# Three expert blocks of a fused attention and mixture-of-experts kernel, rewritten from float32 products into split float32r products

## The chip, the cores and the metric

The kernel runs on one core of one Trainium2 chip. The metric is device time in microseconds of one execution (lower is better). TensorE multiplies and adds into PSUM; ScalarE (ACT in rows), VectorE (DVE) and GpSimd (POOL) do the elementwise work; SyncE (SP) issues most of the transfers. In the rows PE is TensorE's matmuls and PEld its weight loads.

## The reference

Three layers follow each other. The change lies in the second, the top-1 mixture of experts:

```python
# attention: B=2, H=8, S=768, D=64, a query sees the keys of its own cluster -> x: 1536 x 512
logits = x @ w_gate                      # 8 experts
expert_idx = np.argmax(logits, axis=1)
gate_w = softmax(logits)[arange, expert_idx]
for e in range(8):
    mask = expert_idx == e
    h = np.maximum(x[mask] @ w1[e], 0.0) # w1[e]: 512 x 1024
    out[mask] = gate_w[mask, None] * (h @ w2[e])   # w2[e]: 1024 x 512
h = out @ w_in                           # 512 x 2048
g = np.maximum(h, 0) + alpha * np.minimum(h, 0)
return g @ w_out                         # 2048 x 512
```

## The kernel before

The program has three stages: attention, the eight experts, and the dense layer. The tokens of each expert have been gathered into one block. Expert 0 is block 0 (208 rows); the others follow by falling size, with fixed capacities of 306, 216, 200, 192, 176, 168 and 128 rows (`CAPS`). A block is computed transposed: the rows are the columns that a matmul streams, and the weights are what it holds.

The experts run as one loop over steps `g` (`NG` is 64, eight steps `f` to a block). Step g emits `l1(blk, f)`, which makes 128 of the 1024 hidden columns from four products over d, evacuated by a ReLU on ScalarE into `h`; then `l2` of the step two back (`LAG` is 2), which adds that piece of `h` into four PSUM banks; then small side work, at f of 6 the transposes of the next block's rows (`x_transp`), and last the conversions of the dense layer's weights. `l1` has two PSUM banks (`bank(f % 2)`), so step g+2 can't start before the evacuation of step g. At the end of a block `y_evac` copies the four output banks out. The schedule is manual: each engine runs its instructions in the order in which the program emits them.

Operands of the experts are float32; a float32 matmul shows as two records in the trace, each with its own weight load. The dense layer already works with split operands: a value is `hi` (rounded to float32r by a ScalarE copy) plus `lo` (the rest, by a VectorE subtraction), and three float32r products, hi by hi, hi by lo and lo by hi, take the place of one float32 product.

Expert weights arrive as 1 MB chunks, four to a block, in a ring of four slots on SyncE's queue. `wload()` is called when a chunk has been used up and loads the one four places on. The weights of the dense layer arrive as raw 512 KB pieces on the same queue and are converted in steps of one piece (`conv_run`): step k emits the load of piece k, `conv_abs` of piece k-1 (ScalarE, reads the raw piece), `conv_bits` of piece k-2 and `conv_lo` of piece k-4 (VectorE, five instructions), and `conv_hi` of piece k-3 (ScalarE). Two raw buffers exist, so the load of piece k waits for `conv_bits` of piece k-2. The table `PER` says how many conversion steps each block has; the rest (32 pieces, 36 steps) fall one to a step into the start of the dense layer. Their results live in `m2w_t[c]`, pairs of 128x2048 tiles; the first five pairs have memory of their own that is empty until the conversions fill it.

Of the kernel before, what the change touches and what calls it, by code (L numbers as in the profile page):

```python
# [90 lines left out]
def tile_cluster_attention_moe(ctx: ExitStack, tc: tile.TileContext, qk, kk, v, cen, cenr, gate, mw, m2w,  # L91
                               alpha, consts, table, pos, zeros, out):
    nc = tc.nc
# [94 lines left out]
    def conv_run(pool, ks):  # L188

        for k in ks:  # L190
            at = lambda lag: 0 <= k - lag < NCA
# [470 lines left out]
    def at(j, w, f, *a):  # L662
        todo.setdefault((j, w), []).append((f, a))
# [193 lines left out]
    ps = bank(0)[:, 448:448 + E]  # L857
# [169 lines left out]
    def reg(ap, engs, hi):  # L1027
        return nc.values_load(ap, engines=engs, min_val=0, max_val=hi)
# [45 lines left out]


    more = nc.values_load(ovi[0:1, 0, 3:4], min_val=0, max_val=NSEL)
    with tc.For_i(0, more, 1):  # L1077
# [7 lines left out]
        for d in range(4):  # L1085
            ps = bank(2 + d % 2)
# [3 lines left out]
        for f in range(8):  # L1090
# [5 lines left out]
            ps = bank(f % 2)  # L1096
# [169 lines left out]
```

## Time and profile before

| | |
|---|---|
| time, three runs | 716.39, 716.99, 718.03 us (median 716.99) |
| the profiled execution | 717.95 us |
| its span, first to last instruction | 716.2 us |
| TensorE busy (matmul records) | 695.7 us, 97% |
| TensorE weight loads busy | 562.8 us, 79% |
| VectorE busy | 419.0 us, 59% |
| ScalarE busy | 283.5 us, 40% |
| mean granted TensorE clock | 0.989 of full speed |

The profiled execution lies 0.96 us above the median, and 1.75 us of its time are outside the span. A busy share is a mean over three stages with different limits; the expert stage lies between 264 and 446 us of the span, and only it is rewritten. A matmul record's length contains the drain of the array, so what a matmul costs in a stream is the distance between the starts of two records, not the length of one.

### The profile page before, as it was taken

The page shows a single profiled execution, that of the slowest core. Times are in us where ns is not written, and L with a number is a line of the kernel's source. Part 1 is how long each engine was busy: PE and PEld are TensorE (multiplying, and loading weights), DVE is VectorE, ACT ScalarE, POOL GpSimd, SP SyncE. Part 2 cuts the span into 40 slices and gives each one's busy share as a digit, 9 for nine tenths or more (in the row PEclk, how much of TensorE's full clock was granted, in tenths as well). Part 3 has the DMA queues.
Part 4 walks back from the last instruction along what each step waited for, and adds up shares of the span by engine and source line. Part 5 has one row for each costly group of instructions (what it writes and reads, how often), then busy time and mean ns, then how long its engine had stood idle before and what let it go on. Part 6 is the DMA issues. An engine that isn't in the chain of part 4 may idle for free. (4 is left out here: it accounts for less than half of the span.)

```text
span 716.2 us, 10510 instructions
## 1 busy us (share of the span) xinstructions
PE 695.7 (97%) x3966; PEld 562.8 (79%) x3966; DVE 419.0 (59%) x781; ACT 283.5 (40%) x589; POOL 62.4 (9%) x67
## 2 busy tenths in 40 slices
PE   7899999999999999999999998999999999999996
PEld 3676767666667689779999998888888888888885
DVE  7877778788886561686532104799654433543342
ACT  5877877857576412343332213333121111221111
POOL 4220202222220120000000000000002000020002
PEclk8999999999999999999999999899999999999999
DMA  8346667425430027978879775132001000010001
GB/s 268 95 155 190 243 214 243 132 83 135 122 81 1 17 98 224 254 268 273 292 262 260 282 251 121 60 117 89 1 0 60 1 0 1 0 59 1 0 1 59
DMA packets 24763, 89.75 MB, mean 125 GB/s; under 512 B 6818, under 2 KB 8365, under 8 KB 20519
## 3 DMA queue, kind: packets, MB, share of 16 engines
q1 hardware_dynamic: 19515, 72.83, 33.0%
q0 software_dynamic: 3216, 12.60, 5.1%
q10 hardware_dynamic: 1980, 3.63, 1.7%
q8 instruction: 32, 0.52, 0.3%
q14 instruction: 20, 0.16, 0.1%
HBM read 75.06 MB, written 11.35 MB: 121 GB/s over the span
## 5 line engine op out<-in xcount | busy, mean ns | idle before, releaser
L1153 ACT ACTIVATE gh<-gg 128x512 fp32r<-128x512 f32 x48 | 30.4, 632 | 195.7 <-DVE gg L1152 189.5
L401 DVE TENSOR_REDUCE sm<-PS 128x1 f32<-128x768 f32 x96 | 91.9, 957 | 14.9 <-PE PS L395 14.5
L411 ACT ACTIVATE P<-PS,sm 128x768 f32<-128x768 f32 x96 | 86.5, 901 | 32.1 <-DVE sm L401 32.1
L910 PE MATMUL PS<-x,w 128*128 128x208 f32 (+7 forms) x512 | 96.8, 332 | 0.0
L925 PE MATMUL PS<-h,w 128*128 128x208 f32 (+7 forms) x512 | 96.5, 332 | 0.0
L925 PEld LDWEIGHTS PS<-h,w 128*128 128x128 f32 x512 | 83.7, 190 | 4.4
L910 PEld LDWEIGHTS PS<-x,w 128*128 128x128 f32 x512 | 83.7, 190 | 4.2
L425 PEld LDWEIGHTS PS<-cst,P 128*128 128x128 f32 x576 | 63.4, 140 | 29.9 <-ACT P L411 16.8
L425 PE MATMUL PS<-cst,P 128*128 128x128 f32 x576 | 82.6, 278 | 3.3 <-ACT P L411 1.5
L1151 DVE TENSOR_SCALAR gg<-PS,alph 128x512 f32<-128x512 f32 x48 | 36.0, 749 | 80.8 <-PE PS L1143 80.6
L1141 PE MATMUL PS<-x2hi,w2h 128*128 128x512 f32 x192 | 76.0, 396 | 2.7 <-ACT x2hi L1129 2.7
L1142 PE MATMUL PS<-x2lo,w2h 128*128 128x512 f32 x192 | 75.9, 395 | 0.0
L1143 PE MATMUL PS<-x2hi,w2l 128*128 128x512 f32 x192 | 75.7, 394 | 0.0
L428 DVE COPY PT<-PS 128x384 f32<-128x384 f32 x96 | 53.0, 552 | 38.5 <-PE PS L425 38.5
L1170 PE MATMUL PS<-w2h,gh 128*128 128x512 f32 x192 | 74.7, 389 | 0.0
L1171 PE MATMUL PS<-w2l,gh 128*128 128x512 f32 x192 | 74.7, 389 | 0.0
L1172 PE MATMUL PS<-w2h,gl 128*128 128x512 f32 x192 | 74.7, 389 | 0.0
L394 PE MATMUL PS<-KA,QA 128*128 128x512 f32 x192 | 73.8, 384 | 0.0
L434 PE MATMUL PS<-PT,V 128*64 128x384 f32 (+1 forms) x432 | 72.4, 462 | 0.0
L395 PE MATMUL PS<-KB,QB 96*128 96x512 f32 x192 | 61.3, 341 | 0.0
L427 ACT ACTIVATE PT<-PS 128x384 f32<-128x384 f32 x96 | 46.7, 486 | 28.6 <-PE PS L425 27.1
L912 ACT ACTIVATE h<-PS 128x208 f32<-128x208 f32 (+7 forms) x64 | 21.3, 333 | 79.2 <-PE PS L910 79.1
(170 smaller groups left out, 861.9 us busy)
## 6 DMA issues: line engine op xcount, KB each, us to landing
w<-in_mw SPq DMA_DIRECT2D x32, 1024.0 KB, 7.3
raw<-in_m2w SPq DMA_DIRECT2D x32, 512.0 KB, 4.1
R<-in_qk SPq DMA_DIRECT2D x7, 768.0 KB
KA<-in_kk POOLq DMA_DIRECT2D x7, 768.0 KB
Xs<-in_zeros SPq DMA_DIRECT2D x8, 614.4 KB
QA<-QB SPq DMA_DIRECT2D x16, 192.0 KB, 2.6
V<-in_v SPq DMA_DIRECT2D x8, 384.0 KB
KB<-KA SPq DMA_DIRECT2D x7, 384.0 KB, 4.1
```

Source lines behind the costliest of these rows:

```text
L394: nc.tensor.matmul(ps[:, ks], st["QA"][:, hh, q0:q0 + P], st["KA"][:, hh, ks], start=True, stop=False)
L401: nc.vector.tensor_reduce(smt[s], psS[s % 2], AX.X, ALU.max, negate=True)
L411: nc.scalar.activation(Pt, psS[s % 2], AF.Exp, bias=smt.pop(s)[:, 0:1], accum_out=RS[:, tt, h:h + 1])
L425: nc.tensor.transpose(v4[:, kt // 3, kt % 3, :], Pt[:, kt * P:(kt + 1) * P], idf)
L910: nc.tensor.matmul(ps, w[:, d, fs], x[:, d, :], start=d == 0, stop=d == 3)
L925: nc.tensor.matmul(yps[blk][o][:, 0:nb], w[:, f % 4, o * P:(o + 1) * P], h, start=f == 0, stop=f == 7)
L1141: nc.tensor.matmul(ps, whi[:, d, fs], xhi[:, d, :], start=d == 0, stop=False)
L1142: nc.tensor.matmul(ps, whi[:, d, fs], xlo[:, d, :], start=False, stop=False)
L1143: nc.tensor.matmul(ps, wlo[:, d, fs], xhi[:, d, :], start=False, stop=d == 3)
L1170: nc.tensor.matmul(y, gh[:, c], whi[:, f % 4, :], start=f == 0, stop=False)
L1171: nc.tensor.matmul(y, gh[:, c], wlo[:, f % 4, :], start=False, stop=False)
L1172: nc.tensor.matmul(y, gl[:, c], whi[:, f % 4, :], start=False, stop=f == 15)
```

## The change

Block 1 (306 rows) goes from one float32 product to three float32r products. Its four weight chunks are split into hi and lo by `wsplit`, a quarter chunk at a time, into the pairs `m2w_t[1]` to `m2w_t[4]`, at the steps that the table `SPLITS` lists (7 to 13); its rows are split in `x_transp`, its hidden values in `l1s`.

Blocks 2 and 3 (216 and 200 rows) keep the hi and lo halves of their rows side by side, so that one float32r product of hi weights with both halves (432 or 400 columns) and one of lo weights with the hi half (216 or 200 columns) do the work. The two halves of the result are added afterwards, in `l1r` and in `y_evac`. Their weights are split in rolling pieces: `wroll` writes a 128x512 piece of hi and of lo for the next step, into eight pieces that lie in `m2w_t[2][1]` and `m2w_t[3][1]`.

`PER` changes from (3, 8, 4, 3, 2, 1, 0, 2) to (2, 2, 1, 1, 5, 5, 2, 2): 20 conversion steps in the expert stage where there were 23. The weight register of block g+2 is read a block earlier, since chunks are used up sooner. Blocks 0 and 4 to 7 keep their float32 code.

```diff
+        if blk in ROLL:
+            x = xts[blk] = ROLL[blk][0][:, 0:8 * nb].rearrange("p (d s n) -> p d s n", d=4, s=2)
+        elif blk == SPL:
+            xs1[:] = [xtp.tile([P, 4, CMAX], F32R, name=f"x{n}_{blk}", tag="x") for n in ("hi", "lo")]
...
+            if blk in ROLL:
+                xv = x[:, dn * g:dn * (g + 1), :, :]
+                nc.scalar.activation(xv[:, :, 0, :], pv, AF.Copy)
+                nc.vector.tensor_sub(xv[:, :, 1, :], pv, xv.bitcast(F32)[:, :, 0, :])
+            elif blk == SPL:
+                for k in range(dn):
+                    d = dn * g + k
+                    nc.scalar.activation(xs1[0][:, d, 0:nb], pv[:, k], AF.Copy)
+                    nc.vector.tensor_sub(xs1[1][:, d, 0:nb], pv[:, k], xs1[0].bitcast(F32)[:, d, 0:nb])
...
+    def wsplit(k, pieces):
+        hi, lo = m2w_t[1 + k]
+        w = wslots[4 * SPL + k]
+        for i in pieces:
+            c = slice(512 * i, 512 * (i + 1))
+            nc.scalar.activation(hi[:, c], w[:, c], AF.Copy)
+            nc.vector.tensor_sub(lo[:, c], w[:, c], hi.bitcast(F32)[:, c])
+        if pieces[-1] == 3:
+            wload()
+
+    def l1s(f):
...
+        for d in range(4):
+            nc.tensor.matmul(ps, whi[:, d, fs], xhi[:, d, :], start=d == 0, stop=False)
+            nc.tensor.matmul(ps, whi[:, d, fs], xlo[:, d, :], start=False, stop=False)
+            nc.tensor.matmul(ps, wlo[:, d, fs], xhi[:, d, :], start=False, stop=d == 3)
...
+        nc.scalar.activation(hh, ps, AF.Relu)
+        nc.vector.scalar_tensor_tensor(hl, ps, 0.0, hh.bitcast(F32), ALU.max, ALU.subtract)
...
+    ROLL = {2: m2w_t[2], 3: (m2w_t[4][0],)}
+    gran = [m2w_t[2][1][:, 512 * i:512 * (i + 1)] for i in range(4)]
+    gran_lo = [m2w_t[3][1][:, 512 * i:512 * (i + 1)] for i in range(4)]
+    hjoin = m2w_t[3][0]
+
+    def wroll(blk, f, second):
...
+        nc.scalar.activation(hi, src, AF.Copy)
+        nc.vector.tensor_sub(lo, src, hi.bitcast(F32))
+        return hi, lo
...
+    def rolls(g):
+        for n, second in ((g, 0), (g - LAG, 1)):
+            blk, f = divmod(n, 8)
+            if blk in ROLL:
+                rolled[blk, f, second] = wroll(blk, f, second)
+
+    def l1r(blk, f):
...
+            if d < 3:
+                nc.tensor.matmul(ps, hi[:, d, :], x[:, d, :, :], start=d == 0, stop=False)
+                nc.tensor.matmul(ps[:, 0:nb], lo[:, d, :], x[:, d, 0, :], start=False, stop=False)
...
+        h = hp.tile([P, CMAX], F32, name=f"h_{blk}_{f}", tag="h")[:, 0:nb]
+        nc.scalar.activation(h, ps[:, nb:2 * nb], AF.Copy)
+        nc.vector.tensor_add(h, ps[:, 0:nb], h)
...
+        nc.scalar.activation(hh[:, 0, :], h, AF.Relu)
+        nc.vector.scalar_tensor_tensor(hh[:, 1, :], h, 0.0, hh.bitcast(F32)[:, 0, :], ALU.max, ALU.subtract)
...
+            if blk in ROLL:
+                h = hp.tile([P, CMAX], F32, name=f"yl_{blk}_{o}", tag="h")[:, 0:nb]
+                nc.scalar.activation(h, y[:, nb:2 * nb], AF.Copy)
+                nc.vector.tensor_add(dst, y[:, 0:nb], h)
...
-    PER = (3, 8, 4, 3, 2, 1, 0, 2)
+    PER = (2, 2, 1, 1, 5, 5, 2, 2)
+    SPLITS = {7: (0, (0, 1, 2, 3)), 8: (1, (0, 1)), 9: (1, (2, 3)), 10: (2, (0, 1)), 11: (2, (2, 3)), 12: (3, (0, 1)), 13: (3, (2, 3))}
...
+            rolls(g + 1)
             l1(blk, f)
...
+        if g in SPLITS:
+            wsplit(*SPLITS[g])
         conv_run(cvp, conv_steps(g))
```

In the program's order the change is seen best at three places. The first is VectorE at the seam between blocks 1 and 2. Before, steps 14 and 15 hold block 2's row copy and one conversion each; in L175 and its like the names `cv` and `raw` are a piece under conversion.

```order
L899 COPY x_3195<-PS 128x2x216
L186 TENSOR_TENSOR w2l_2702<-cv_3124,w2h_2701 128x512
L173 TENSOR_SCALAR cv_3181<-cv_3181 128x512
L174 TENSOR_SCALAR cv_3181<-cv_3181 128x512
L175 SCALAR_TENSOR_TENSOR cv_3181<-raw_3146,cv_3181 128x512
L176 SCALAR_TENSOR_TENSOR cv_3181<-raw_3146,cv_3181 128x512
```

Now (`w2l` and `w2h` are the lo and hi tiles of the pairs in `m2w_t`, here in their second use; L904 splits block 2's rows, L975 is the lo half of `wroll`):

```order
L941 SCALAR_TENSOR_TENSOR hlo_3282<-PS,hhi_3281 128x306
L904 TENSOR_TENSOR w2h_2703<-PS,w2h_2703 128x2x216 x2
L975 TENSOR_TENSOR w2l_2706<-w_3052,w2l_2704 128x512
L941 SCALAR_TENSOR_TENSOR hlo_3324<-PS,hhi_3323 128x306
L173 TENSOR_SCALAR cv_3184<-cv_3184 128x512
L174 TENSOR_SCALAR cv_3184<-cv_3184 128x512
L175 SCALAR_TENSOR_TENSOR cv_3184<-raw_3006,cv_3184 128x512
L176 SCALAR_TENSOR_TENSOR cv_3184<-raw_3006,cv_3184 128x512
L975 TENSOR_TENSOR w2l_2706<-w_3052,w2l_2704 128x512
L1000 TENSOR_TENSOR h_0_3358<-PS,h_0_3358 128x216
L1004 SCALAR_TENSOR_TENSOR w2h_2705<-h_0_3358,w2h_2705 128x216
```

The first L975 stands behind the two L904; it writes into the tile `w2l_2706`. On TensorE the last L1 step of block 1 reads that same tile, in its third product (L938), right behind the transposes (L899):

```order
L899 MATMUL PS<-cst,xr_3078 128x108 x8
L936 MATMUL PS<-xhi_2960,w2h_2705 128x306
L937 MATMUL PS<-xlo_2961,w2h_2705 128x306
L938 MATMUL PS<-xhi_2960,w2l_2706 128x306
```

So the third product of that step has moved behind an L975, and with it behind the two row splits L904.

The second place is one step of block 2 in its middle, on VectorE. Before, such a step held one conversion or nothing; this is step 21:

```order
L186 TENSOR_TENSOR w2l_2704<-cv_3234,w2h_2703 128x512
L173 TENSOR_SCALAR cv_3355<-cv_3355 128x512
L174 TENSOR_SCALAR cv_3355<-cv_3355 128x512
L175 SCALAR_TENSOR_TENSOR cv_3355<-raw_3296,cv_3355 128x512
L176 SCALAR_TENSOR_TENSOR cv_3355<-raw_3296,cv_3355 128x512
```

Now steps 21 and 22 (L1000 adds the two halves of the L1 result, L1004 makes the lo half of h):

```order
L975 TENSOR_TENSOR w2l_2706<-w_3178,w2l_2704 128x512
L975 TENSOR_TENSOR w2l_2706<-w_3267,w2l_2704 128x512
L1000 TENSOR_TENSOR h_5_3554<-PS,h_5_3554 128x216
L1004 SCALAR_TENSOR_TENSOR w2h_2705<-h_5_3554,w2h_2705 128x216
L975 TENSOR_TENSOR w2l_2706<-w_3178,w2l_2704 128x512
L975 TENSOR_TENSOR w2l_2706<-w_3267,w2l_2704 128x512
L1000 TENSOR_TENSOR h_6_3581<-PS,h_6_3581 128x216
L1004 SCALAR_TENSOR_TENSOR w2h_2705<-h_6_3581,w2h_2705 128x216
L904 TENSOR_TENSOR w2h_2707<-PS,w2h_2707 128x2x200 x2
L975 TENSOR_TENSOR w2l_2706<-w_3503,w2l_2704 128x512
```

Each step now has four instructions on VectorE, and on ScalarE four that alternate with them (L974 twice, L999 ahead of L1000, L1003 between L1000 and L1004); both steps' conversions are gone from here.

The third place is ScalarE in block 4, whose own code is unchanged. Before, steps 34 to 39, with `conv_hi` (L183), `conv_abs` (L168) and the ReLUs (L912):

```order
L912 ACTIVATE h_3_3699<-PS 128x192
L183 ACTIVATE w2h_2705<-cv_3568 128x512
L168 ACTIVATE cv_3713<-raw_3613 128x512
L912 ACTIVATE h_4_3721<-PS 128x192
L912 ACTIVATE h_5_3731<-PS 128x192
L912 ACTIVATE h_6_3743<-PS 128x192
L897 ACTIVATE x_3749<-PS 128x2x176
L912 ACTIVATE h_7_3764<-PS 128x192
L183 ACTIVATE w2h_2707<-cv_3611 128x512
L168 ACTIVATE cv_3778<-raw_3715 128x512
```

Now the same steps (the ReLUs are L1040):

```order
L1040 ACTIVATE h_3_4038<-PS 128x192
L183 ACTIVATE w2h_2701<-cv_3922 128x512
L168 ACTIVATE cv_4052<-raw_4000 128x512
L1040 ACTIVATE h_4_4060<-PS 128x192
L183 ACTIVATE w2h_2701<-cv_3998 128x512
L168 ACTIVATE cv_4072<-raw_4054 128x512
L1040 ACTIVATE h_5_4080<-PS 128x192
L1040 ACTIVATE h_6_4092<-PS 128x192
L911 ACTIVATE x_4098<-PS 128x2x176
L183 ACTIVATE w2h_2701<-cv_4052 128x512
L168 ACTIVATE cv_4115<-raw_4074 128x512
L1040 ACTIVATE h_7_4123<-PS 128x192
```

There are four conversion steps where there were two, and two pairs of them are one step apart.

## Rows read from the trace of the kernel before

**Rows 1.** Busy time by stretch, blocks 1 to 5 (stretch, length; engines; clock; DMA share, GB/s)

```profile
285.70:318.10 32.40, 32.40 (x137) 24.74 (x136) 24.21 (x60) 11.78 (x24) 0.00 (x0) 1.00 0.82 256
318.10:343.40 25.30, 25.30 (x138) 24.15 (x137) 16.35 (x40) 9.86 (x22) 0.00 (x0) 1.00 0.89 287
343.40:366.00 22.60, 22.60 (x138) 22.57 (x138) 9.55 (x18) 7.22 (x17) 0.00 (x0) 1.00 0.85 275
366.00:387.50 21.50, 21.50 (x137) 21.48 (x136) 6.73 (x14) 6.19 (x16) 0.00 (x0) 1.00 0.84 257
387.50:407.40 19.90, 19.90 (x138) 19.89 (x137) 3.76 (x9) 4.56 (x14) 0.00 (x0) 1.00 0.75 259
```

**Rows 2.** Waits in the expert stage (us in total, times, longest)

```profile
ACT cv L168 <- DMA raw<-in_m2w: 31.0, 12, 6.2
```

**Rows 3.** Timeline of TensorE at five places (start, length, engine, line, operation)

```profile
285.68 2.23 PE L910 MATMUL PS<-x,w 128*128 128x306 f32 x8
...
287.74 1.57 PE L925 MATMUL PS<-h,w 128*128 128x208 f32 x8
...
326.62 1.62 PE L925 MATMUL PS<-h,w 128*128 128x216 f32 x8
328.08 1.62 PE L910 MATMUL PS<-x,w 128*128 128x216 f32 x8
...
101.48 0.28 PE L394 MATMUL PS<-KA,QA 128*128 128x256 f32 x1
101.60 0.29 PE L395 MATMUL PS<-KB,QB 96*128 96x256 f32 x1
...
500.08 0.39 PE L1142 MATMUL PS<-x2lo,w2h 128*128 128x512 f32 x1
501.44 0.39 PE L1171 MATMUL PS<-w2l,gh 128*128 128x512 f32 x1
...
249.33 1.86 PE L477 MATMUL PS<-G,OT 128*128 128x16 f32 x16
```

**Rows 4.** Weight loads by form (busy us, mean ns of one)

```profile
L1142 PEld LDWEIGHTS PS<-x2lo,w2h 128*128 128x128 f32 x192 | 36.7, 191 | 8.1 <-DVE x2lo L1130 0.4
...
L477 PEld LDWEIGHTS PS<-G,OT 128*128 128x128 f32 x24 | 2.9, 191 | 0.0
```

**Rows 5.** ScalarE and VectorE by form, 264.4 to 470 us

```profile
L183 ACT ACTIVATE w2h<-cv 128x512 fp32r<-128x512 f32 x24 | 15.0, 624 | 3.0 <-DVE cv L173 1.5 <-DVE x2b L936 0.9 <-DVE cv L176 0.4
...
L912 ACT ACTIVATE h<-PS 128x216 f32<-128x216 f32 x8 | 2.7, 342 | 3.7 <-PE PS L910 3.6
...
L186 DVE TENSOR_TENSOR w2l<-cv,w2h 128x512 fp32r<-128x512 f32 x23 | 15.7, 684 | 0.5 <-ACT w2h L183 0.2 <-ACT h L912 0.2
...
L899 DVE COPY x<-PS 128x432 f32<-128x432 f32 x1 | 0.6, 609 | 0.0
L936 DVE COPY x2a<-PS 128x216 f32 x1 | 0.4, 384 | 4.4 <-PE PS L925 4.4
```

**Rows 6.** Timelines of VectorE and ScalarE where equal work follows itself

```profile
305.36 0.69 DVE L176 SCALAR_TENSOR_TENSOR cv<-raw,cv 128x512 int32<-128x512 int32 x1
305.96 0.68 DVE L186 TENSOR_TENSOR w2l<-cv,w2h 128x512 fp32r<-128x512 f32 x1
...
444.98 1.15 ACT L1129 ACTIVATE x2hi<-x2a 128x512 fp32r<-128x512 f32 x2 [1.93 <-issue]
```

**Rows 7.** Transfers by line (KB each, median us from issue to landing)

```profile
w<-in_mw SPq DMA_DIRECT2D x32, 1024.0 KB, 7.3
raw<-in_m2w SPq DMA_DIRECT2D x32, 512.0 KB, 4.1
```

**Rows 8.** Busy time by stretch, eight microseconds inside the expert stage

```profile
382.00:390.00 8.00, 8.00 (x55) 7.98 (x55) 3.28 (x6) 2.52 (x6) 0.00 (x0) 1.00 0.95 347
```

**Rows 9.** The start of the dense layer: timeline of TensorE, and a stretch

```profile
445.66 0.79 PE L1141 MATMUL PS<-x2hi,w2h 128*128 128x512 f32 x1 [2.71 <-ACT x2hi L1129]
...
445.60:448.00 2.40, 2.34 (x5) 1.61 (x6) 2.36 (x4) 1.57 (x4) 0.00 (x0) 0.50 0.31 4
```

More of the change, by code (lines that the diff above doesn't have):

```diff
@@ L899, in x_transp @@
                 nc.vector.tensor_copy(x[:, dn * g:dn * (g + 1), :], pv)
-        xts[blk] = x
+    SPL = 1
+    xs1 = []
+    def wsplit(k, pieces):
[8 more added lines that the diff above has]
+    def l1s(f):
+        nb = CAPS[SPL]
+        whi, wlo = (t.rearrange("p (d f) -> p d f", d=4) for t in m2w_t[1 + 2 * (f // 4)])
+        xhi, xlo = (t[:, :, 0:nb] for t in xs1)
+        ps = bank(f % 2)[:, 0:nb]
+        fs = slice((f % 4) * P, (f % 4 + 1) * P)
+        for d in range(4):
+            nc.tensor.matmul(ps, whi[:, d, fs], xhi[:, d, :], start=d == 0, stop=False)
+            nc.tensor.matmul(ps, whi[:, d, fs], xlo[:, d, :], start=False, stop=False)
+            nc.tensor.matmul(ps, wlo[:, d, fs], xhi[:, d, :], start=False, stop=d == 3)
+        hh, hl = (hp.tile([P, CMAX], F32R, name=f"h{n}_{f}", tag="h")[:, 0:nb] for n in ("hi", "lo"))
+        nc.scalar.activation(hh, ps, AF.Relu)
+        nc.vector.scalar_tensor_tensor(hl, ps, 0.0, hh.bitcast(F32), ALU.max, ALU.subtract)
+        hts[SPL, f] = hh, hl
@@ new lines, in l2s @@
+    def l2s(f):
+        nb = CAPS[SPL]
+        whi, wlo = (t.rearrange("p (f d) -> p f d", f=4)[:, f % 4] for t in m2w_t[2 + 2 * (f // 4)])
+        hh, hl = hts.pop((SPL, f))
+        if f == 0:
+            yps[SPL] = [bank(4 + o) for o in range(4)]
+        for o in range(4):
+            y, os = yps[SPL][o][:, 0:nb], slice(o * P, (o + 1) * P)
+            nc.tensor.matmul(y, whi[:, os], hh, start=f == 0, stop=False)
+            nc.tensor.matmul(y, whi[:, os], hl, start=False, stop=False)
+            nc.tensor.matmul(y, wlo[:, os], hh, start=False, stop=f == 7)
@@ new lines, in tile_cluster_attention_moe @@
+    ROLL = {2: m2w_t[2], 3: (m2w_t[4][0],)}
[3 more added lines that the diff above has]
+    def wroll(blk, f, second):
+        w = wslots[4 * blk + 2 * (f // 4) + second]
+        hi = gran[2 * second + f % 2]
+        if second:
+            src = w[:, 512 * (f % 4):512 * (f % 4 + 1)]
+        else:
+            src = w.rearrange("p (d f) -> p d f", d=4)[:, :, (f % 4) * P:(f % 4 + 1) * P]
+            hi = hi.rearrange("p (d f) -> p d f", d=4)
+        lo = gran_lo[2 * second + f % 2]
+        if not second:
+            lo = lo.rearrange("p (d f) -> p d f", d=4)
+        nc.scalar.activation(hi, src, AF.Copy)
+        nc.vector.tensor_sub(lo, src, hi.bitcast(F32))
+        return hi, lo
@@ new lines, in tile_cluster_attention_moe @@
+    rolled = {}
+    def rolls(g):
[4 more added lines that the diff above has]
+    def l1r(blk, f):
+        nb = CAPS[blk]
+        hi, lo = rolled.pop((blk, f, 0))
+        x = xts[blk]
+        ps = bank(f % 2)[:, 0:2 * nb]
+        for d in range(4):
+            if d < 3:
+                nc.tensor.matmul(ps, hi[:, d, :], x[:, d, :, :], start=d == 0, stop=False)
+                nc.tensor.matmul(ps[:, 0:nb], lo[:, d, :], x[:, d, 0, :], start=False, stop=False)
+            else:
+                nc.tensor.matmul(ps[:, 0:nb], lo[:, d, :], x[:, d, 0, :], start=False, stop=False)
+                nc.tensor.matmul(ps, hi[:, d, :], x[:, d, :, :], start=False, stop=True)
+        h = hp.tile([P, CMAX], F32, name=f"h_{blk}_{f}", tag="h")[:, 0:nb]
+        nc.scalar.activation(h, ps[:, nb:2 * nb], AF.Copy)
+        nc.vector.tensor_add(h, ps[:, 0:nb], h)
+        i = f % 4
+        hh = hjoin[:, 2 * nb * i:2 * nb * (i + 1)].rearrange("p (s n) -> p s n", s=2)
+        nc.scalar.activation(hh[:, 0, :], h, AF.Relu)
+        nc.vector.scalar_tensor_tensor(hh[:, 1, :], h, 0.0, hh.bitcast(F32)[:, 0, :], ALU.max, ALU.subtract)
+        hts[blk, f] = hh
+        if f % 4 == 3:
+            wload()
@@ new lines, in l2r @@
+    def l2r(blk, f):
+        nb = CAPS[blk]
+        hi, lo = rolled.pop((blk, f, 1))
+        hh = hts.pop((blk, f))
+        if f == 0:
+            yps[blk] = [bank(4 + o) for o in range(4)]
+        for o in range(4):
+            y, os = yps[blk][o], slice(o * P, (o + 1) * P)
+            if f < 7:
+                nc.tensor.matmul(y[:, 0:2 * nb], hi[:, os], hh, start=f == 0, stop=False)
+                nc.tensor.matmul(y[:, 0:nb], lo[:, os], hh[:, 0, :], start=False, stop=False)
+            else:
+                nc.tensor.matmul(y[:, 0:nb], lo[:, os], hh[:, 0, :], start=False, stop=False)
+                nc.tensor.matmul(y[:, 0:2 * nb], hi[:, os], hh, start=False, stop=True)
+        if f % 4 == 3:
+            wload()
@@ L917, in l2 @@
     def l2(blk, f):
+        if blk == SPL:
+            return l2s(f)
+        if blk in ROLL:
+            return l2r(blk, f)
         nb = CAPS[blk]
@@ L1060, in tile_cluster_attention_moe @@
             if f == 1 and blk + 1 < NB:
-                wreg[blk + 1] = reg(wi[0:1, blk + 1:blk + 2], [ET.SP], 4 * (E - 1))
+                for b_ in range(blk + 1, min(blk + 3, NB)):
+                    if b_ not in wreg:
+                        wreg[b_] = reg(wi[0:1, b_:b_ + 1], [ET.SP], 4 * (E - 1))
                 row = reg(rowi[0:1, blk + 1:blk + 2], [ET.Activation], E * N - N)
```

17 lines of the change are left out of this document (12 added, 5 removed).

## The prediction

> **What bounds the kernel now.** I read the busy time by stretch first. In blocks 1 to 5 TensorE is busy in every microsecond (32.40 of 32.40 us in block 1), at the full clock, while VectorE works 24.2, 16.4, 9.6, 6.7 and 3.8 us of the five stretches and the transfers run at 256 to 287 GB/s [rows 1]. The reader is to see two things: the expert stage is a TensorE stage, and the spare time of the other engines grows from block to block. Then I read TensorE's timeline for the distance from matmul to matmul, the forms of ScalarE and VectorE for the price of an added instruction, and the waits and the transfers for what a conversion step needs. ScalarE waits for raw pieces 12 times, 31.0 us in all and 6.2 us once [rows 2], and TensorE feels none of it.
>
> **What TensorE saves.** A float32 record of 306 columns costs 2.06 us for eight, 0.2575 us each; of 216 columns 1.46 for eight, 0.1825 [rows 3], and by columns 0.169 at 200. A float32r product of 256 columns costs 0.12, one of 512 costs 0.227 (six in 1.36 us) [rows 3]; on the line through both, 306 columns cost 0.141, 400 cost 0.180 and 432 cost 0.193. No float32r product under 256 columns is in the trace. The nearest row from below is 16 float32 records of 16 columns in 1.86 us, 0.116 each with the last one's drain [rows 3]: with next to nothing to stream, the weight load is the floor, and the loads of float32r and of float32 are equally long, 191 ns [rows 4]. From above bounds it what the float32 product costs there, two records, 0.365. I take 0.115 for 216 and 200 columns, since the 256-column product at 0.12 is the nearest row in kind and size.
> - Block 1: 128 x 0.2575 = 33.0 us become 192 x 0.141 = 27.1: -5.9.
> - Block 2: 64 x 0.365 = 23.4 become 64 x (0.193 + 0.115) = 19.7: -3.7.
> - Block 3: 64 x 0.338 = 21.6 become 64 x (0.180 + 0.115) = 18.9: -2.7.
>
> Together -12.3 us. This holds only while the operands are ready.
>
> **What it adds around block 1: +3.8.** A 128x512 half costs ScalarE 0.624 and VectorE 0.684 [rows 5]; where equal work follows itself, the next starts 0.60 later on VectorE and 0.53 later on ScalarE (1.15 for two) [rows 6]. At the start of block 1 all four pieces of the first chunk are split behind the last ReLU of block 0: about 0.4 for that ReLU, 0.62 + 3 x 0.53 for the copies, 0.68 for the last lo, 3.3 us in all. TensorE has eight records of L2 (1.4) and eleven products (1.5) to do; with three restarts at the earlier pieces 0.8 are lost. The row banks of block 1 are now freed by a copy and a subtraction in turn where one did it: 0.5. The second half of the weights repeats the start with two pieces: 0.5. At the end of block 1 the third product of its last L1 step waits for the first piece that `wroll` makes for block 2, since both use one tile. That piece stands behind the two row splits, and those behind the transposes just ahead: two copies of 432 columns (0.5 and 0.4), the weight copy (0.55), the subtraction (0.7) and a restart (0.15) are 2.3 us, of which two products hide 0.3: 2.0.
>
> **What it adds in blocks 2 and 3: +6.5.** In a step ScalarE and VectorE hand over four times: two weight copies, two subtractions, copy of one half, add, ReLU, subtraction. With ScalarE's first copy at 0 the subtractions end at 1.33 and 1.93, the add (like the 216-column copy, 0.384 [rows 5]) at 2.23, the ReLU (0.342 [rows 5]) at 2.6, and the next step's first copy can start at 2.5. A step of 2.53 us stands against 8 x 0.308 = 2.46 and 8 x 0.295 = 2.36 of TensorE. The steps alone lose 8 x 0.07 + 8 x 0.17 = 1.9 us; that is the lower end. Between them VectorE also has two conversions (2.85 each: 0.60 for the L186, 0.45 twice, 0.7 twice), eight additions of the output behind copies (3), the split of block 3's rows (1, from 0.609 for 432 columns [rows 5]), block 1's output (0.9) and the small table work (2), 12.6 us; on top of 1.9 the upper end is 14.5. The two banks of L1 let TensorE run a step ahead, so each of three bunches (the table work, the seams behind blocks 2 and 3) can hide some 2.4: 7. I take 6.5. This is a choice by the counting of slack; no row shows it.
>
> **What it adds in blocks 4 and 5: +3.5.** These blocks get ten conversion steps for three. A step's raw load is issued after its VectorE work (2.85), takes 4.1 us [rows 7], and `conv_abs` of the next conversion step waits for it on ScalarE, with the ReLUs of later steps behind it. Where two conversion steps follow each other (twice in each block) the raw piece is wanted after one step of TensorE, 16 x 0.162 = 2.6 us, and comes at 6.9; the ReLU two steps on is done at about 8.4 with 0.67 for the conversion and 0.5 for the start. TensorE needs it 3.5 steps on, at 9.1 in block 4 and 8.3 in block 5. So there is hardly slack, and what a raw piece comes later than 4.1 us is paid in full. It will come later: four chunks, five raw pieces and the next rows are 7.2 MB, in 20.8 us 345 GB/s and in 19.1 us 375, against 347 in the best eight microseconds [rows 8] and 257 to 287 over whole blocks [rows 1]. I take 0.9 us for each of the four pairs. The lower end is 0: in block 1 the waits of [rows 2] cost TensorE nothing. The upper end is 14.4 MB at 287 GB/s, 50 us where the blocks have 40; less 2 for what the ring has loaded ahead: 8.
>
> **What costs nothing.** The dense layer gets 16 conversion steps for 13. Its step is 24 x 0.227 = 5.4 us of TensorE; VectorE has eight instructions, three of its own at 0.7 and the five at 2.85, 5.0: hidden. A weight half that misses its step would cost one, 5.4. The registers read earlier have a block's time.
>
> **The sum.** -12.3 + 3.8 + 6.5 + 3.5 = +1.5. The profiled execution of 717.95 us (span 716.2, 1.75 outside) would become 719.45; it stood 0.96 above the median of 716.99, so I forecast 718.5.
>
> **A rule weighed.** [rows 3] have products 0.12 apart whose loads last 0.19 [rows 4]: the loads overlap each other, and their busy time is no bound. The Trainium skill, Perfetto Trace Analysis, section Identifying the Most-Contended Engine, wants the headroom of TensorE judged by the busy share of LDWEIGHTS. Summed as if loads could not overlap, 192 x 0.191 = 36.7 us would replace block 1's 33.0 and 128 x 0.191 = 24.4 each replace 23.4 and 21.6: +7.5 instead of -12.3.
>
> **The rivals.**
> - *The raw pieces stay hidden* (0.24). As in block 1 now [rows 2], blocks 4 and 5 lose nothing: 718.5 - 3.5 = 715.0, faster. For it: two banks and two steps of lag. Against it: 345 GB/s. It decides at raw pieces landing within some 4.5 us.
> - *VectorE and ScalarE keep up in blocks 2 and 3* (0.10): 2 lost for 6.5, raw pieces 2 for 3.5, 712.5. For it: the average step is only 0.1 too long.
> - *They don't, and the banks hide little* (0.10): 13 for 6.5, 725.
> - *Narrow float32r products are not one short pass* (0.12). At the float32 record's 0.1825 (0.07), TensorE has 7.8 more, half of it inside the stalls: 722.5. At float32's 0.365 (0.05), 64 x (0.25 + 0.22) = 30 more, less the 6.5 of stalls: 742. For it: no such row exists.
> - *Loads bound the blocks* (0.02): from -12.3 to +7.5, with 8 of the stalls covered, 730. Against it: [rows 3, 4]. This is the mechanism that the skill's metric implies.
>
> **How the numbers follow.** The forecast has 0.42, with 716 to 721 as its own range. The range 712.5 to 723.5 leaves out half of the fast case, most of the slow one and the wide float32r prices, some 0.19. A measurement of this kernel tells a change of 0.2% (1.4 us) from none: faster is under 715.6 (the fast case, two thirds of the hidden one, little of the forecast: 0.30), slower over 718.4 (half of the forecast, and the three slow cases: 0.42), the same 0.28.
>
> **What would show it.** Right: matmuls of 306 columns about 0.14 apart and narrow ones 0.115; one TensorE stall of 2 us at the end of block 1 that waits for L975; blocks 2 and 3 together near 47 us with stalls of 0.2 to 1.5 released by VectorE; ScalarE waiting for raw pieces in blocks 4 and 5 and TensorE for ScalarE. Wrong: narrow products 0.18 or more apart; blocks 2 and 3 in 41 us or in 53; no TensorE stall in blocks 4 and 5. A lower clock would also break it: after the 2.71 us of idle time ahead of the dense layer the granted clock is 0.50, which is 1.2 GHz [rows 9]; if a stall of 2 us brought that on inside the blocks, several microseconds more would go.

## The result, and the profile after

The changed kernel takes 726.13 us (median of four runs, 723.4 to 727.23) against 717.36 us before: the ratio is 1.0132, 95% interval 1.0108 to 1.0156. It is 8.8 us slower; 718.5 was forecast, and 726.13 is outside the range. The profiled execution is the fastest of the four, 723.4 us with a span of 721.6; two of the others had a lower mean clock (0.986 and 0.984 for 0.991) and took 727.1 and 727.2. So the profile shows less of the loss than the medians: 5.4 us of span.

First the busy time by stretch, blocks 0 to 6 (from the first L1 matmul of a block to that of the next; columns as in [rows 1]):

```profile
262.98:284.88 21.90, 21.13 (x127) 20.65 (x125) 4.88 (x21) 5.07 (x15) 1.57 (x3) 1.00 0.56 180
284.88:315.87 30.99, 29.00 (x193) 27.61 (x193) 21.96 (x56) 15.42 (x33) 0.00 (x0) 1.00 0.79 250
315.87:339.06 23.19, 21.99 (x147) 20.89 (x145) 18.51 (x47) 13.91 (x34) 0.00 (x0) 1.00 0.45 144
339.06:363.96 24.90, 21.59 (x139) 19.49 (x137) 20.07 (x43) 15.59 (x40) 0.00 (x0) 1.00 0.70 214
363.96:391.23 27.27, 23.40 (x138) 22.91 (x137) 19.27 (x39) 11.11 (x26) 0.00 (x0) 0.94 0.73 239
391.23:415.73 24.50, 22.38 (x139) 21.65 (x138) 14.96 (x28) 8.72 (x21) 0.00 (x0) 0.93 0.83 287
415.73:434.51 18.78, 18.78 (x134) 18.78 (x133) 6.32 (x14) 5.39 (x16) 0.00 (x0) 1.00 0.95 301
```

The reader is to compare TensorE's busy time with the length. In [rows 1] they were equal in each of blocks 1 to 5; now only block 6 is like that. Block 1 is 1.4 us shorter and blocks 2 and 3 together are as long as before, although TensorE has less to do there. Blocks 4 and 5, whose products did not change, take 27.3 and 24.5 us where they took 21.6 and 19.9: that is the loss, 10.3 us. There the mean clock is below 1 for the first time, and in block 2 the transfers run at only 144 GB/s.

The timeline of ScalarE and of TensorE inside block 4 shows one such stall (in brackets the idle time ahead, and what ended it):

```profile
379.03 0.67 ACT L168 ACTIVATE cv<-raw 128x512 f32<-128x512 f32 x1 [4.10 <-DMA raw<-in_m2w]
...
385.91 0.67 ACT L168 ACTIVATE cv<-raw 128x512 f32<-128x512 f32 x1 [5.47 <-DMA raw<-in_m2w]
386.47 0.55 ACT L1040 ACTIVATE h<-PS 128x192 f32<-128x192 f32 x2
...
382.93 0.77 PE L899 MATMUL PS<-cst,xr 88*128 88x88 f32 x8
386.85 2.14 PE L1038 MATMUL PS<-x,w 128*128 128x192 f32 x8 [3.15 <-ACT h L1040]
```

`conv_abs` at 385.91 has waited 5.47 us for a raw piece; two ReLUs stand behind it in ScalarE's order, and TensorE needs the first of them for the bank of its next L1 step. SyncE's timeline gives the age of that piece:

```profile
373.80 0.34 SPq L164 DMA_DIRECT2D raw<-in_m2w  x1
...
375.56 0.34 SPq L144 DMA_DIRECT2D w<-in_mw  x1
376.69 5.78 SPq L164 DMA_DIRECT2D raw<-in_m2w  x2
```

It is the first of the two loads of the last line, issued at 376.69: 9.2 us from issue to use, where [rows 7] had a median of 4.1 to landing. The chunk issued 1.1 us ahead of it was late as well: it landed after 9.0 us (transfers by line, 370 to 392 us; only one of the three has its landing in the trace), 1.3 us before the piece was used.

```profile
w<-in_mw SPq DMA_DIRECT2D x3, 1024.0 KB, 9.0
```

Around the two long stalls the granted clock is at 0.50 for a while, which is 1.2 GHz (the view by stretch again, cut to the low clock):

```profile
387.70:391.10 3.40, 3.40 (x13) 3.40 (x12) 3.28 (x6) 1.61 (x4) 0.00 (x0) 0.50 0.48 165
411.60:415.00 3.40, 3.40 (x12) 3.40 (x13) 3.26 (x7) 2.35 (x6) 0.00 (x0) 0.50 0.83 318
```

Each costs half of its 3.4 us. The stalls of blocks 4 and 5 (3.15 and 1.85), the two low-clock stretches (3.4 together) and 0.72 us that the last L2 step of block 3 waits make 9.1 of the 10.3; the rest is not traced.

The waits of the expert stage by engine show the rest of what was foretold:

```profile
ACT cv L168 <- DMA raw<-in_m2w: 30.0, 9, 5.7
...
PE PS L1038 <- ACT h L1040: 5.0, 2, 3.2
...
PE PS L994 <- DVE w2l L975: 2.7, 3, 1.2
...
PE PS L938 <- DVE w2l L975: 1.8, 1, 1.8
```

ScalarE's total for raw pieces is what it was in [rows 2], 30.0 us for 31.0; but it now falls into short steps. Two differences outside the blocks were not foretold, and both help the profiled run: the expert stage began 1.4 us earlier, and the dense layer's start, which had the half clock from 445.1 to 451.9 us ([rows 9] show its first part), kept the full clock behind an idle time of 2.41 us, which is 2.5 us less for its first step. So 9.4 us in the expert stage became 5.4 of span. Where the other 3.4 us between the medians lie was not profiled.

### The profile page after: what moved, and what is told of

Same layout as the page of the kernel before. It is cut to its first block, busy times and chain, and to the rows that moved or that the text cites. A ratio compares the mean times of both kernels' runs of the same rounds, so it can differ in the third digit from the quotient of the medians.

```text
span 721.6 us, 10817 instructions
## 1 busy us (share of the span) xinstructions
PE 688.5 (95%) x4030; PEld 560.5 (78%) x4030; DVE 466.8 (65%) x877; ACT 315.0 (44%) x661; POOL 61.3 (9%) x67
## 5 line engine op out<-in xcount | busy, mean ns | idle before, releaser
L1038 PE MATMUL PS<-x,w 128*128 128x208 f32 (+4 forms) x320 | 56.0, 320 | 5.3 <-ACT h L1040 5.0
L1057 PE MATMUL PS<-h,w 128*128 128x208 f32 (+4 forms) x320 | 55.2, 318 | 0.0
L1038 PEld LDWEIGHTS PS<-x,w 128*128 128x128 f32 x320 | 50.3, 195 | 6.2 <-ACT h L1040 6.2
L1057 PEld LDWEIGHTS PS<-h,w 128*128 128x128 f32 x320 | 50.7, 196 | 0.0
L1327 POOL DMA_INDIRECT out_dram<-row,PGR x12 | 11.6, 970 | 441.1 <-ACT row L1324 438.4
```

## The experiments

All time is against the kernel before, run beside each. Block lengths are read from TensorE's timeline of the profiled run, as above; block 7 is left out.

| kernel | time / before (us) | ratio, 95% interval | blocks 0 to 6 (us) |
|---|---|---|---|
| before | | | 21.3, 32.4, 25.3, 22.6, 21.6, 19.9, 18.8 |
| changed | 726.13 / 717.36 | 1.0132, 1.0108 to 1.0156 | 21.9, 31.0, 23.2, 24.9, 27.3, 24.5, 18.8 |
| e1 before, PER changed | 725.46 / 716.18 | 1.0101, 1.0049 to 1.0154 | 21.3, 32.4, 25.3, 22.6, 23.4, 24.6, 22.7 |
| e2 steps spread | 726.05 / 716.18 | 1.0141, 1.0105 to 1.0176 | 21.9, 32.3, 23.3, 24.9, 22.2, 20.9, 24.8 |
| e3 no raw loads | 715.81 / 716.18 | 0.9996, 0.9979 to 1.0012 | 21.9, 31.0, 23.2, 25.1, 22.2, 19.9, 18.8 |
| e4 block 1 only | 723.00 / 716.18 | 1.0097, 1.0059 to 1.0136 | 21.9, 29.0, 24.6, 22.6, 23.8, 24.4, 20.4 |
| e5 block 1, early steps | 720.59 / 716.75 | 1.0063, 1.0045 to 1.0081 | 21.9, 32.5, 25.7, 22.6, 21.6, 19.9, 18.8 |
| e6 all, early steps | 730.33 / 716.75 | 1.0191, 1.0174 to 1.0208 | 21.9, 32.5, 29.0, 33.5, 22.2, 19.9, 18.8 |
| e7 = e3, late roll | 714.60 / 716.75 | 0.9977, 0.9964 to 0.9990 | 21.9, 29.0, 23.8, 24.9, 22.2, 19.9, 18.8 |
| e8 raw, other queue | 731.39 / 716.75 | 1.0210, 1.0193 to 1.0227 | 21.9, 31.0, 23.2, 25.6, 25.7, 26.7, 21.1 |
| e9 block 1, spaced | 715.07 / 716.75 | 0.9982, 0.9961 to 1.0003 | 21.8, 29.0, 24.6, 22.6, 21.6, 19.9, 18.8 |
| e10 before, spaced | 716.39 / 716.75 | 0.9996, 0.9976 to 1.0015 | 21.3, 32.4, 25.3, 23.3, 21.6, 19.9, 18.8 |
| e11 = e7, no roll lo | 707.73 / 716.75 | 0.9882, 0.9852 to 0.9911 | 21.9, 29.0, 21.4, 20.9, 21.2, 19.9, 18.8 |
| e12 = e7, lo on GpSimd | 712.91 / 716.82 | 0.9942, 0.9924 to 0.9959 | 21.9, 29.0, 23.3, 25.4, 21.4, 19.9, 18.8 |
| e13 all, three remedies | 729.46 / 716.82 | 1.0186, 1.0134 to 1.0238 | 24.8, 29.0, 27.1, 31.8, 21.2, 19.9, 20.1 |

**e1: the table of conversion steps alone, in the kernel before.**

```diff
-    PER = (3, 8, 4, 3, 2, 1, 0, 2)
+    PER = (2, 2, 1, 1, 5, 5, 2, 2)
```

> The kernel before, with nothing changed but the table PER = (2, 2, 1, 1, 5, 5, 2, 2). Theory R (conversion steps): in the changed kernel blocks 4 and 5 took 27.3 and 24.5 us for 21.6 and 19.9, because ten conversion steps stand there, two of them one step apart twice in each block; ScalarE waits for the raw piece, the ReLUs stand behind it, and each TensorE stall of 1.9 to 3.2 us is followed by a half-clock spell of 3.4 us. Then this kernel loses the same in the same blocks: 5 to 10 us there, 722 to 727 in all, though it has no float32r block. Theory V (the ring): the transfers of blocks 4 and 5 are late because the float32r blocks free the chunk slots at other times. Then this kernel stays within 1.5 us of 717.

Measured: 9.3 us slower by the times and 7.2 by the ratio; its four runs lie between 719.8 and 729.0 us, and the profiled one is the slowest. Its stretches of blocks 3 to 6:

```profile
344.02:366.58 22.56, 22.56 (x137) 22.53 (x137) 3.91 (x8) 4.85 (x14) 0.00 (x0) 1.00 0.76 229
366.58:389.99 23.41, 22.05 (x137) 21.56 (x137) 13.66 (x26) 7.69 (x19) 0.00 (x0) 1.00 0.80 258
389.99:414.54 24.55, 20.70 (x139) 19.96 (x137) 15.00 (x29) 8.62 (x22) 0.00 (x0) 1.00 0.89 297
414.54:437.28 22.74, 20.72 (x134) 20.45 (x133) 8.22 (x17) 6.40 (x19) 0.00 (x0) 0.92 0.83 285
```

Blocks 0 to 3 are as before to 0.1 us; blocks 4 to 6 lose 1.9, 4.6 and 4.0, 10.4 together, and no float32r block is in the kernel. So theory V is not needed: the table alone does it. The waits are the same pair, ScalarE for the raw piece and TensorE for ScalarE:

```profile
ACT cv L168 <- DMA raw<-in_m2w: 29.5, 9, 5.2
...
PE PS L910 <- ACT h L912: 7.2, 6, 2.0
```

**e2: as many steps, none directly behind another.**

```diff
-    PER = (2, 2, 1, 1, 5, 5, 2, 2)
+    PER = (2, 2, 1, 1, 3, 4, 4, 3)
```

> The changed kernel with PER = (2, 2, 1, 1, 3, 4, 4, 3): as many conversion steps, none a step behind another in blocks 4 to 7. R: the stalls of 3.2 and 1.9 us and both half-clock spells go, 8 to 10 us less than the changed kernel, 716 to 718; blocks 6 and 7 lose less than 1. V: no change beyond 2 us, about 725.

Nothing came back, and this part of R is wrong. Blocks 4 and 5 lose under a microsecond each now, but block 6 loses 6.1, in one stall of 4.0 us with the low clock behind it. ScalarE's timeline there:

```profile
417.94 0.62 ACT L183 ACTIVATE w2h<-cv 128x512 fp32r<-128x512 f32 x1
426.50 0.66 ACT L168 ACTIVATE cv<-raw 128x512 f32<-128x512 f32 x1 [7.93 <-DMA raw<-in_m2w]
427.06 0.49 ACT L1040 ACTIVATE h<-PS 128x168 f32<-128x168 f32 x2
```

That piece was issued at 417.58, and the conversions are two steps apart. Steps one behind the other are not needed for the stall: a piece that takes 8.9 us is late for a distance of two steps as well, when these are 2.3 us long.

**e3: without the ten raw loads of blocks 4 and 5** (ScalarE's and VectorE's conversions stay, on old data).

```diff
+        if 6 <= n < 16:
+            raws[n] = raws[n - 1]
+            return
```

> The changed kernel without the loads of raw pieces 6 to 15, the ten that fall in blocks 4 and 5; their conversions run on piece 5's data, so part of the dense weights are not the reference's. Engine work and order stay. R with the transfer as the cause: blocks 4 and 5 go back to 21.6 and 19.9 us, 716 in all. If ScalarE's and VectorE's conversion work itself holds up the ReLUs, at least 4 of the 10 us stay.

The ratio to the kernel before falls from 1.0132 to 0.9996, some 9.8 us, and blocks 4 and 5 are back to 22.2 (0.7 of it the wait of block 3's last step) and 19.9. It is the load of the pieces that holds things up, not the conversion work.

**e4: block 1 only.**

```diff
-    ROLL = {2: m2w_t[2], 3: (m2w_t[4][0],)}
+    ROLL = {}
```

> The changed kernel with blocks 2 and 3 back in float32 (ROLL empty); block 1 split, PER as changed. By the profile of the changed kernel blocks 2 and 3 together took 48.1 us for 47.8, so float32r there gains nothing: 725 to 727, the same as the changed kernel, with 5 to 10 us lost in blocks 4 and 5 still (R). If the rolled blocks cost more in runs that were not profiled, or feed the late transfers (V): 720 or less.

By the ratios 2.5 us under the changed kernel, between the two expectations. Blocks 4 to 6 lose 8.3 us (R stands), block 1 takes 29.0 without the wait for `wroll`, and blocks 2 and 3 take 47.1 in float32, less than the 48.1 with float32r: the rewriting of these two is a net loss.

**e5: block 1 only, and the conversion steps early.**

```diff
-    PER = (2, 2, 1, 1, 5, 5, 2, 2)
+    PER = (2, 3, 5, 4, 3, 2, 1, 2)
```

> Block 1 alone in three products (ROLL empty), and the conversion steps back where the transfers had room: PER = (2, 3, 5, 4, 3, 2, 1, 2). R: in e4 the blocks 1 to 3 took 76.1 us for 80.3 and block 0 0.6 more, and all that was lost stood in blocks 4 to 7; with at most three conversion steps in each of those, the gain is left: 3 to 4 us under the kernel before, 712 to 714. If five and four conversion steps in blocks 2 and 3 wait for raw pieces as they did in blocks 4 and 5, or the split of block 1 costs the later blocks something of its own: 716 or more.

Blocks 4 to 6 are as before to 0.1 us, as R said. But other things took the gain: in block 1 a stall of 2.04 us (the product L938 waits for L925, which stands behind the conversion of step 10 and the table work of step 11 on VectorE) with the low clock behind it, in block 2 a stall of 0.88 us behind a raw piece that ScalarE waited 6.70 us for, and 5.12 us of idle time ahead of the dense layer, told of at the end. So with five conversion steps in a block of 3.1 us a step, late pieces cost something there too.

**e6: the whole change, steps early.**

```diff
-    PER = (2, 2, 1, 1, 5, 5, 2, 2)
+    PER = (2, 2, 3, 4, 3, 3, 2, 1)
```

> The changed kernel with PER = (2, 2, 3, 4, 3, 3, 2, 1): five more conversion steps in blocks 2 and 3, where the transfers ran at 144 and 214 GB/s, five fewer in blocks 4 to 7. R: blocks 4 to 7 lose under 2 us, but the conversions add 2.9 us each to VectorE and 1.3 to ScalarE in the two blocks where those hand over four times a step, 1 to 3 us more there: 717 to 720. If those two engines have no room at all in blocks 2 and 3: 724 or more.

Blocks 4 to 6 lose 0.6 in all, and blocks 2 and 3 take 62.4 us for 48.1: VectorE and ScalarE have no room there, as the second expectation says; part of it is the clock, which was at 0.50 for 11.7 us of the two. So in the tables tried, the pieces could be loaded neither late nor early beside the rolled blocks.

**e7: e3 with the first rolled piece behind the last L1 step of block 1.**

```diff
-            rolls(g + 1)
+            if g != 15:
+                rolls(g + 1)
             l1(blk, f)
+            if g == 15:
+                rolls(g + 1)
```

> The kernel of e3 (without the loads of raw pieces 6 to 15) with the first wroll piece of block 2 emitted behind the last L1 step of block 1, so that the third product of that step has nothing to wait for. If the stall of 1.77 us ahead of L938 is that conflict over one tile: 1.5 to 2 us less than e3, 714, the stall gone. If the two row splits and the weight piece were late anyway, the stall moves to the first step of block 2 and the time stays within 0.7 us of e3's 715.8.

1.2 us under e3 by the times, 1.4 by the ratios, a little less than the 1.5 foretold; the stall ahead of the third product is gone (TensorE's timeline, the last L1 step of block 1, of the changed kernel and then of e7):

```profile
310.58 0.30 PE L937 MATMUL PS<-xlo,w2h 128*128 128x306 f32 x1
312.65 0.41 PE L938 MATMUL PS<-xhi,w2l 128*128 128x306 f32 x1 [1.77 <-DVE w2l L975]
```

```profile
311.15 0.30 PE L940 MATMUL PS<-xlo,w2h 128*128 128x306 f32 x1
311.29 0.31 PE L941 MATMUL PS<-xhi,w2l 128*128 128x306 f32 x1
```

Block 1 gives back 2.0 us, of which block 2 takes 0.6.

**e8: the raw pieces on GpSimd's queue.**

```diff
-        nc.sync.dma_start(raws[n].rearrange("p n t -> p (n t)"), ...)
+        eng = nc.gpsimd if 6 <= n < 20 else nc.sync
+        eng.dma_start(raws[n].rearrange("p n t -> p (n t)"), ...)
```

> The changed kernel with the loads of raw pieces 6 to 19 issued by GpSimd on its own queue, no longer on SyncE's behind the 1 MB chunks. If a raw piece is late because it stands behind a chunk in one queue: the 5 to 9 us from issue to use become 4 or so, and 4 to 8 us come back, 718 to 722. If the transfers as a whole are short in blocks 4 and 5 (the bytes, R): within 2 us of 726, since chunks and pieces share the same engines.

By the ratios 5.6 us slower than the changed kernel. The first such load is issued at 375.82 and its piece is used at 384.22, 8.4 us later. So another queue does not make the pieces earlier. That the chunk ahead plays no part is not shown by it. SyncE issued one at 375.42, and the transfers by queue (packets, MB, share; q0 is GpSimd's queue, q1 SyncE's, q10 ScalarE's) show, from 376.8 to 381.9 us, the chunk moving and nothing on q0:

```profile
q1 hardware_dynamic: 132, 0.97, 64.4%
q10 hardware_dynamic: 6, 0.00, 0.5%
```

From 381.9 to 384.6 us two pieces, both issued before 378.7, moved at once:

```profile
q0 software_dynamic: 262, 0.99, 89.5%
q1 hardware_dynamic: 31, 0.12, 11.6%
```

Whether they waited for the chunk, or GpSimd's queue was late by itself, these rows do not tell; ScalarE's queue was not tried.

**e9 and e10: block 1 only with spaced steps, and the same table in the kernel before.**

```diff
-    PER = (2, 2, 1, 1, 5, 5, 2, 2)
+    PER = (3, 2, 4, 4, 3, 2, 2, 2)
```

> Block 1 alone in three products, PER = (3, 2, 4, 4, 3, 2, 2, 2): 22 conversion steps, two in block 1 (at f of 3 and 7, clear of the table work that held up e5 there), none a step behind another. R: block 1 in 29.0 us as in e4, block 2 in 24.6 to 25.0, blocks 3 to 7 as before: the expert stage 3.0 to 3.5 us shorter than before's 181.3. If TensorE's branch ahead of the dense layer takes 0.3 to 1 us: 713 to 714.5; if it takes 3.3 as in e5, with the gap of 5.1 us and the half-clock spell behind it: 716 to 718.

> The kernel before with the same table PER = (3, 2, 4, 4, 3, 2, 2, 2) and no float32r block: what of e9 is the table's. R: nothing, within 1 us of the kernel before, since no conversion step is within 4.3 us of the last. If these tables alone give or cost something: more than 1.5 us either way.

e9 comes out at 715.07, 1.7 us under the kernel before, with an interval that still holds 1, so a gain is not shown by the time; e10 is not to be told from the kernel before, so the table itself gives nothing. e9's blocks 1 to 4:

```profile
285.61:314.61 29.00, 28.78 (x194) 27.63 (x193) 22.78 (x58) 14.47 (x30) 0.00 (x0) 1.00 0.83 269
314.61:339.16 24.55, 24.55 (x146) 24.51 (x145) 15.89 (x39) 8.41 (x19) 0.00 (x0) 1.00 0.66 180
339.16:361.72 22.56, 22.56 (x137) 22.53 (x137) 12.49 (x24) 8.21 (x19) 0.00 (x0) 1.00 0.90 308
361.72:383.27 21.55, 21.55 (x138) 21.53 (x137) 9.53 (x19) 7.25 (x17) 0.00 (x0) 1.00 0.88 276
```

TensorE is busy throughout. 3.7 us are gained up to the start of block 7; some 1.2 of them go ahead of the dense layer.

**e11 and e12: who is the limit in blocks 2 and 3.** Both are e7 with one line of `wroll` changed, in e11 left out, in e12:

```diff
-        nc.vector.tensor_sub(lo, src, hi.bitcast(F32))
+        (nc.gpsimd if second else nc.vector).tensor_sub(lo, src, hi.bitcast(F32))
```

> The kernel of e7 without the subtractions of wroll (the lo weights of blocks 2 and 3 keep old data). If VectorE and ScalarE handing over in turn is what holds blocks 2 and 3 (a step of 2.53 us, of which the two subtractions are about 0.5 to 0.6 on the path): the stalls of 1.19, 1.08 and 1.19 us there go, blocks 2 and 3 take 45 to 46 us for 48.7, 3 us under e7. If ScalarE alone (two weight copies, half copy, ReLU) is the limit: within 1 us of e7.

> The kernel of e7 (no loads of raw pieces 6 to 15, first wroll piece late) with the subtraction of wroll's second piece, the one for L2, on GpSimd. A GpSimd subtraction of 64x768 took 1.89 us in the profile of before, so one of 512 columns is estimated at 1.3 by columns. Theory S (VectorE's subtractions in the hand-over are the limit, as e11 says): about half of e11's 6.9 us come back, 2.5 to 4.5 us under e7, 710 to 712. If the subtraction's result is simply needed by L2 sooner than any engine has it, or GpSimd and VectorE slow each other: within 1.5 us of e7's 714.6.

Blocks 2 and 3 of e7, then of e11:

```profile
314.43:338.24 23.81, 22.39 (x147) 20.86 (x145) 19.21 (x49) 14.30 (x34) 0.00 (x0) 1.00 0.48 152
338.24:363.15 24.91, 21.58 (x138) 19.49 (x137) 20.08 (x43) 15.60 (x40) 0.00 (x0) 1.00 0.71 215
```

```profile
315.26:336.63 21.37, 21.37 (x146) 20.88 (x145) 11.11 (x34) 14.92 (x35) 0.00 (x0) 1.00 0.53 168
336.63:357.50 20.87, 20.14 (x138) 19.56 (x137) 10.26 (x26) 15.66 (x39) 0.00 (x0) 1.00 0.81 263
```

Without VectorE's subtractions the two blocks are 6.5 us shorter and TensorE is busy throughout block 2; ScalarE's work is the same, 30.6 us for 29.9. That is twice what was expected, and ScalarE alone is not the limit. Without the subtractions VectorE also works 17.9 us less there (21.4 for 39.3), so e11 does not tell the handing over from VectorE's load. With half of the subtractions on GpSimd 1.7 us come back by the times and 2.5 by the ratios, at or under the low end of what was expected. A subtraction takes 1.34 us there, VectorE's own grow meanwhile (from 0.69 to 0.79 us for 128x512), and of the first pieces, which stayed on VectorE, two are now 1.6 and 2.2 us late; around the second the clock is 0.50 for 6.8 us, of which TensorE works 6.0: some 3.0 lost.

**e13: the whole change with the three remedies** (e7's late piece, e12's line, and this table).

```diff
-    PER = (2, 2, 1, 1, 5, 5, 2, 2)
+    PER = (4, 2, 2, 3, 3, 3, 2, 1)
```

> The whole change with its three costs treated: first wroll piece behind the last L1 step of block 1, wroll's second subtraction on GpSimd, PER = (4, 2, 2, 3, 3, 3, 2, 1), so that blocks 4 to 7 hold nine conversion steps. R and S together: blocks 4 to 7 as before (one us more at most), blocks 2 and 3 with five conversion steps 47 to 49 us, block 1 29: 711 to 715, at or under the kernel before. If the conversions crowd VectorE in blocks 2 and 3 as in e6 (62 us there): 718 or more.

Blocks 4 and 5 are as before and block 1 takes 29.0, but five conversion steps in blocks 2 and 3 make them 58.8 us, block 0 loses 2.9 against the changed kernel to a wait of 2.0 for the row split and the low clock behind it, and block 6 loses 1.3, of it 1.0 to a chunk that is late. None of the forms of the whole change that do all of the work (the changed kernel, e2, e6, e8, e13) was faster than the kernel before; e7, e11 and e12 leave out loads.

## Why the prediction was wrong

**The step that failed is blocks 4 and 5.** "I take 0.9 us for each of the four pairs", 3.5 in all and 8 at most, became 10.3: 5.0 us in two stalls, 3.4 for the clock, and 0.7 at the seam. The mechanism was the one named (raw piece, `conv_abs`, the ReLUs behind it, TensorE's bank), and e1 and e3 show it alone: the table without the change costs 9.3 us by the times and 7.2 by the ratio, the change without the loads is as fast as the kernel before. Three things in the sizing were wrong. A raw piece that ScalarE waits for takes 4.8 to 9.2 us from issue to use there, not 4.1 and a little; that median [rows 7] is of the six loads, of 32, whose landing the trace has. The loads that ScalarE waited longest for in the kernel before had taken as long (296.21 to 303.00 us, and 333.25 to 340.75, below). The loss was tied to pairs of steps, and e2 shows that it is not. And the price of the clock, put only under what would break the forecast, belonged in the sum: 3.4 of the 10.3 us.

Why [rows 2] misled: in block 1 of the kernel before the same waits of up to 6.2 us cost nothing, since a step there lasts 4.05 us (32.4 over eight). In blocks 4 to 6 it lasts 2.7 to 2.3, and the two steps of cover shrink with it. This is argued from the lengths; no run changed the length of a step alone. The rival "the raw pieces stay hidden" rested on that row.

**What held.** A product of 306 columns follows the last by 0.14 us; 432 and 216 columns together take 0.305 (0.308 in the sum), 400 and 200 take 0.295 (0.295). TensorE's timeline in block 2 of the changed kernel, start by start:

```profile
325.66 0.26 PE L1019 MATMUL PS<-w2h,w2l 128*128 128x216 f32 x1
325.76 0.37 PE L1018 MATMUL PS<-w2h,w2l 128*128 128x432 f32 x1
325.97 0.26 PE L1019 MATMUL PS<-w2h,w2l 128*128 128x216 f32 x1
326.06 0.37 PE L1018 MATMUL PS<-w2h,w2l 128*128 128x432 f32 x1
```

The narrow one alone shows 0.10 and the wide one 0.21; only the pair is what was priced. The rivals on dear narrow products and on weight loads fall. By the loads' lengths summed block 1 would have taken 36.7 us; e9's 29.0 contradicts that reading of the rule that judges TensorE's headroom by the busy share of its weight loads (the Trainium skill, Perfetto Trace Analysis, section Identifying the Most-Contended Engine). The share of the time in which some load ran was high all the same, 27.63 of 29.00 us.

Around block 1, 3.8 us of stalls were foretold, in four places, and each is there: for the row banks 0.77 (L899 waits for the row split L909) against 0.5, for the first step 1.1 against 0.8 (twelve products in 2.77 us), for the second half 0.5, and for the rolled piece 2.1 with its restart against 2.0. The net of blocks 0 and 1 is -0.9 us where -2.1 was summed; block 1's last two L2 steps, which fall into block 2's stretch, add -0.7 (block 2 of e4 against that of the kernel before). In blocks 2 and 3 -6.4 + 6.5 = +0.1 was summed. Their stretches are 0.25 longer than before, and 1.0 longer than in e4, where block 1 is split too. e11 ties the loss to VectorE's subtractions, 6.5 us without them. That the sum had this number is in part luck: it was a choice between 1.9 and 14.5, and its own counting, 14.5 less 7, gives 7.5.

**What stays open.** Why a raw piece takes up to 9 us was not settled. Another queue does not help (e8). It is not peculiar to the changed kernel: in block 2 of the kernel before a piece took 7.5 us from issue to use, and TensorE did not stall (SyncE's timeline, then ScalarE's):

```profile
333.25 0.33 SPq L164 DMA_DIRECT2D raw<-in_m2w  x1
```

```profile
340.75 0.67 ACT L168 ACTIVATE cv<-raw 128x512 f32<-128x512 f32 x1 [4.24 <-DMA raw<-in_m2w]
```

The mean rate alone does not decide either, since that block ran at 287 GB/s [rows 1], as much as block 5 of the changed kernel.

## What to carry to other kernels

When a change takes over memory that a side job used, price the side job where it goes: here the products cost what was summed, and the ten loads in the blocks that they moved to cost the kernel most. Cover is counted in steps but lasts in microseconds, so a wait that is free in a long block is no evidence for a short one. And a wait for a transfer that is put ahead of a ReLU in ScalarE's order can reach TensorE: here 5.47 us of the one became 3.15 of the other. What a stall costs is its length and, often, a stretch at half clock on top.

## What the runs showed that was not expected

The low clock does not follow from a stall's length alone. A stall of 2.0 us in e1 was followed by 3.4 us at 0.50, one of 3.3 us in block 4 of e8 was not. The one of 1.77 us at the end of block 1 was not in the changed kernel, and was in e2, which has the same code there (both views by stretch, the changed kernel and then e2):

```profile
312.70:320.00 7.30, 7.30 (x50) 7.23 (x51) 4.60 (x11) 3.81 (x8) 0.00 (x0) 1.00 0.34 109
```

```profile
315.00:318.40 3.40, 3.40 (x16) 3.37 (x14) 2.62 (x6) 2.03 (x4) 0.00 (x0) 0.50 0.04 17
```

Ahead of the dense layer TensorE passes a branch (the skipped overflow loop). Its longest branch instruction took 0.31 us in the kernel before, e1 and e10, 0.41 in the changed one, 2.1 in e9, 3.3 in e5 and 3.9 in e4, and the idle time there grew to 3.9, 5.1 and 5.7 us. The row of e5 (count, then shortest, median and longest in ns):

```profile
L1221 PEldq COMPARE_BRANCH  x3: 97/193/3285, 442.1 to 448.4; - x3
```

Each is from one profiled execution. What decides it was not tried. In e9 it takes back some 1.2 of the 3.7 us gained.
